# First attention batch pooled by TensorE from the local blocks' tiles, and the float64 words' shift on either of two engines

## The chip, the cores and the metric

The kernel runs on 1 core of one Trainium2 chip. The metric is the device time of one execution in microseconds (us). Engine names are short: PE is TensorE (PEld its weight loads), DVE is VectorE, ACT is ScalarE, POOL is GpSimd, SP is SyncE, whose queue starts the transfers (SPq).

## What is computed

Three parts follow each other; the output of one is the input of the next. The weights come as float64, and the kernel makes float32 of them itself.

```python
def attention(q, k, v):            # (4, 8, 576, 64); 4 batches, 8 heads, 576 tokens, 64 wide
    # pooled: mean of every 4 tokens of q, k, v, full softmax over 144 x 144, each row given to 4 tokens
    out_up = np.repeat(sm_attn(pool4(q), pool4(k), pool4(v)), 4, axis=2)
    # local: full resolution, but only keys at a distance under 4
    scores = np.where(np.abs(i - j) < 4, scale * q @ k.T, -1e9)
    return out_up + softmax(scores) @ v

def mixture1(x, w_in, w_out):      # x (2304, 512), w_in (512, 2048), w_out (2048, 512)
    h = x @ w_in
    return (h * np.cos(h)) @ w_out

def mixture2(x, w_gate, w_val, w_out, rms_g):   # 512 -> 1536 -> 512
    xn = x / rms(x) * rms_g
    return (silu(xn @ w_gate) * (xn @ w_val)) @ w_out
```

## The kernel before

The kernel is written as some hundred generators. A planner (`Order`, in the kernel itself) runs them while the program is built: each `yield` names an engine and an assumed duration, waits for an event, or takes a buffer from a pool, and the planner picks which generator issues next. What runs on the chip is the fixed order per engine that comes out, so an engine works strictly in that order and stands still when its next instruction waits. Where a `yield` lists two engines, the planner chooses the one that would be done first (a number behind an engine is a handicap).

**Attention, batch 0** (`start`, `pq_first`, `pv`, `pooled`, `block`, `block_v`). The pooled part has its own loads: q and k come in six pieces `pq` (tokens on all 128 partitions, four neighbours in a row; `pq_src`). The sums over four are made by DVE for q (L385) and in two adds by POOL for k (L380, L382), then PE transposes them (L425) and ACT writes them into the tiles `pqs` (L401). The pooled v has four loads `v` of its own (L480, L483), summed by POOL (L504 to L511) into `vh` and `vhl`. `pooled` makes the scores of a pair of heads (`sps`, L539), the softmax (L544 to L560), a transposition (`tra`, L575) and the product with v (`avp`, L594), whose result goes to `od` (L602).

The local part works in five blocks of 116 tokens. `block` loads the block's q and k (`raw`, L798, 256 KB each), transposes them (`btr`, L646, 4 instructions in the program for each), makes the scores (`bs`, L684, L690), the softmax (L699 to L712), a transposition (`bat`, L726), and the product with v (`bav`, L752) from the tiles `vb` (L814, four transfers of 64 KB a block, three buffers). L762 adds `od`, so no block can be finished ahead of the pooled part. L775 (ACT) and L777 (POOL) write the result into the tiles `big` as the two halves of x that mixture 1 reads. Batches 1 to 3 take the same path later, with tiles of their own (`rqk`, `pq`).

**Weights of mixture 1** (`w_loads`, `w_conv`). 32 pieces of 512 KB are loaded as pairs of 32-bit words (`rawwa`, `rawwb`, L291 and L293). A piece is converted in five steps: L316 on DVE shifts the low words right by 29, L320 on ACT rescales the high words, L322 on DVE puts both together, L324 on ACT makes the high half `wwa`/`wwb`, and L327 on POOL or DVE the low half.

**Mixture 1** (`unit`, `second`). x has nine tiles of 256 tokens. Tile 0 needs blocks 0 and 1 and the first 24 tokens of block 2; tile 1 needs the rest of batch 0 up to token 511; tile 2 the end of block 4 and the first two blocks of batch 1. A unit is two products `h` (L1013, 12 instructions each), the cosine (L1031 to L1049, ACT, DVE and POOL) and two products `y` (L1079, 6 instructions for each of two halves). Tiles 0 and 1 are run interleaved, 64 groups `h` and `y` together; each pair of units needs four weight pieces. `keep_warm` (L251) fills times in which the planner sees PE idle with products `warm` that nobody reads. Mixture 2 starts after that; its 36 weight pieces go through the same five steps in `w2_conv`.

`LOADS` sets the order of the first transfers on SP, after the six `pq`: four weight pieces, one block's q and k, the four `v`, one block, four weight pieces, three blocks.

Of the kernel before, what the change touches and what calls it, by code (L numbers as in the profile page):

```python
# [9 lines left out]
F32 = mybir.dt.float32  # L10
F32R = mybir.dt.float32r
I32 = mybir.dt.int32
ACTF = mybir.ActivationFunctionType
ALU = mybir.AluOpType
# [22 lines left out]
NQK, NV = 2, 3  # L37
LOADS = (("w", 4), ("r", 1), ("v", 0), ("r", 1), ("w", 4), ("r", 3))
# [11 lines left out]
NQS = 1  # L50
CVB, GLB = 9, 0.5
# [141 lines left out]
def fused_kernel(ctx: ExitStack, tc, q, k, v, w_in, w_out, w_gate, w_val, w_out2, rms_g, mask, bmask, out):  # L193
# [109 lines left out]

    def w_conv(m, i, raw, rp, r):
# [5 lines left out]
        w = p[1] if p[2] == "wg" else p[0].tile([128, 2, 512], F32R, tag=p[1], name="w" + p[1])  # L310
        raw = raw.rearrange("p (b c) -> p b c", c=2)
# [3 lines left out]
        a = yield "DVE", 0.34  # L315
        DVE.tensor_scalar(out=lw, in0=lw, scalar1=29, scalar2=None, op0=ALU.logical_shift_right)  # L316


# [57 lines left out]
    def sum4(b, w, t, o, n):  # L376

        if b or w:
            yield "POOL", 0.05 + n * 0.32
            POOL.tensor_tensor(out=t[:, :n, 0:2], in0=t[:, :n, 0:2], in1=t[:, :n, 2:4], op=ALU.add)  # L380
            yield "POOL", 0.05 + n * 0.18
            POOL.tensor_tensor(out=o, in0=t[:, :n, 0], in1=t[:, :n, 1], op=ALU.add)  # L382
        else:
            yield "DVE", 0.05 + n * 0.27
            DVE.tensor_reduce(out=o, in_=t[:, :n].rearrange("p u r d -> p u d r"), axis=AX.X, op=ALU.add)  # L385
# [28 lines left out]
    def pq_first(w, c, t, qs, place):  # L414

        u0, n = UC[c]
        yield wait(("pq", w, c))
        yield from sum4(0, w, t, qs[:, u0:u0 + n], n)
        give("pqp", place)
        yield take("att")  # L420
        i = yield take("bank")
        ps = bank_tile(i, [64, 4, 128], "trq")
        yield "PE", 0.2 * n
        for x in range(n):
            PE.transpose(ps[:, x, :], qs[:, u0 + x, :], ident)  # L425
        yield from pq_ev(0, w, c, ps)
        give("bank", i)
        give("att", "att")
        count(("pq", 0), 6)
# [57 lines left out]
    def pv(b, hp, t=None, place=None, vh=None):  # L487

        vi = 0
        if b == 0:  # L490
            yield wait(("pv", hp))
        else:
            vi = yield take("vh")
            vh = VH[vi]
            p = []
            for _ in range(2):
                x = yield take("pq")
                p.append(x)
            t = (ap.tile([128, 512], F32, tag=p[0], name="v4").rearrange("p (c x) -> p c x", c=2),
                 ap.tile([128, 512], F32, tag=p[1], name="v4")[:, :256])  # L500
            yield from pv_load(b, hp, *t)
# [10 lines left out]
        if b == 0:  # L512
            give(place[2], place)
        else:
            for x in p:
                give("pq", x)
# [3 lines left out]
    def pooled(b, hp, E=None):  # L520
# [72 lines left out]
        for c in range(3):  # L593
            PE.matmul(o, vh[:, c], A[:, c], start=c == 0, stop=c == 2)  # L594
# [35 lines left out]
    def block(b, u, raw, pools):  # L630
# [9 lines left out]
        for w in range(2):  # L640
# [4 lines left out]
            for a in range(4):  # L645
                PE.transpose(t[:, a, :], raw[w][:, 2 * a:2 * a + 2].rearrange("t h d -> t (h d)"), ident)  # L646
# [107 lines left out]
        give("vb", v_i)  # L754
# [46 lines left out]

    def block_v():

        for b in range(B):
            for u in range(5):
                S_.due(blk_due(b, u) - 5.0)
                x = yield take("vb")
                VI[b, u] = x
                r0 = geo(u)[2]
                vp = v[b].rearrange("(a e) t d -> e t a d", e=2)  # L810
                for s, (_, _, kc) in enumerate(groups(u)):
                    for e in range(2):
                        yield "SP", 0.5
                        SP.dma_start(VB[x][64 * e:64 * e + 64, s], vp[e, r0 + kc:r0 + kc + 64])  # L814
                done(("rv", b, u))
# [26 lines left out]
    def start():  # L842
# [3 lines left out]
        for n in [("pq", w, c) for c in range(3) for w in range(2)] + [("qs", w) for w in range(2)] + [("E", hp) for hp in (1, 2, 3)] \  # L846
                + [("v4", hp) for hp in range(4)] + [("vhl", 0)] + [("raw", u) for u in range(5)]:
            pl[n] = yield take(PLACES)
# [4 lines left out]
        def load(ev, us):  # L853
            yield "SP", us

        qs = [early(("qs", w), [128, 9, 64]) for w in range(2)]
        for c, (u0, n) in enumerate(UC):
            for w in range(2):
                t = early(("pq", w, c), [128, 4, 4, 64])
                yield "SP", max(0.48, 0.37 * n)  # L860
                SP.dma_start(t[:, :n], pq_src(0, w, u0, n))
                done(("pq", w, c))
                S_.add(pq_first(w, c, t, qs[w], pl["pq", w, c]), 0.0, S_.now())
# [984 lines left out]
```

## Time and profile before

| | us |
|---|---|
| runs (3), median | 983.76 (983.52 to 984.35) |
| the profiled execution, its own time | 984.96 |
| span of its records | 983.1 |
| PE busy | 953.0 (97% of the span) |
| DVE busy | 721.2 (73%) |
| ACT busy | 542.3 (55%) |
| POOL busy | 269.1 (27%) |

The span runs from the first to the last record of the execution; 1.9 us of its own time lie outside. Busy time of PE counts the products `warm` too, so it is not the same as useful work. Durations further on come from this one execution.

### The profile page before, as it was taken

What the parts mean: (1) busy time and instruction counts of PE and PEld (TensorE: products, weight loads), DVE (VectorE), ACT (ScalarE), POOL (GpSimd) and SP (SyncE); (2) the same over time, 40 slices, a digit from 0 to 9 for tenths busy, and PEclk for the clock granted to TensorE, in tenths of its full rate; (3) what the DMA queues carried; (4) which work ended last, traced back from release to release, by engine and by line L of the source; (5) the groups of instructions that cost most, each with busy time, mean ns of one, the idle gap of its engine ahead of it and who ended that gap; (6) DMA issues with size and microseconds to landing.
All of it is one profiled execution on the core that took longest, in us unless ns stands there. A gap on an engine that the chain in (4) does not pass through costs nothing.

```text
span 983.1 us, 19205 instructions
## 1 busy us (share of the span) xinstructions
PE 953.0 (97%) x7150; PEld 880.4 (90%) x7150; DVE 721.2 (73%) x1460; ACT 542.3 (55%) x1090; POOL 269.1 (27%) x325
## 2 busy tenths in 40 slices
PE   6789899999999999999999999999999999999998
PEld 6688778888988888888888889999999999999998
DVE  2789976677657775666577699586666688999895
ACT  3658886677677965656566465242322334554442
POOL 3877685544336311101042242000000014300000
PEclk9999999999999999999999999999999999999999
DMA  8788643567685554544331311133222144454432
GB/s 241 212 211 246 181 147 111 148 199 180 199 231 166 170 171 128 176 144 169 120 129 65 107 44 49 49 106 93 75 82 71 57 145 132 132 174 139 141 119 76
DMA packets 160333, 136.07 MB, mean 138 GB/s; under 512 B 72176, under 2 KB 133744, under 8 KB 160240
## 3 DMA queue, kind: packets, MB, share of 16 engines
q1 hardware_dynamic: 160240, 134.85, 45.8%
q8 instruction: 56, 0.92, 0.4%
q14 instruction: 37, 0.30, 0.1%
HBM read 98.64 MB, written 36.18 MB: 137 GB/s over the span
## 4 chain that ended last, share of the span: by engine, by line
PE 84%; DMA 4%; DVE 3%; SPq 3%; issue 2%; POOL 2%; ACT 2%; DVEq 0%; POOLq 0%; ACTq 0%
PE gvp L1502 26%; PE y L1079 19%; PE h L1013 18%; PE o L1755 13%; PE bav L752 2%; PE btr L646 1%; DMA pq<-in_q 1%; DMA raw<-in_k 1%; PE avp L594 1%; PE bs L690 1%; PE yt L1407 1%; POOL wwa L327 1%; PE bat L726 1%; PE sps L539 1%; DMA cst<-in_moe_rms_g 1%
## 5 line engine op out<-in xcount | busy, mean ns | idle before, releaser
L1502 PE MATMUL gvp<-xc,wc 128*128 128x384 f32 x1296 | 231.7, 335 | 0.0
L1502 PEld LDWEIGHTS gvp<-xc,wc 128*128 128x128 f32 x1296 | 225.6, 188 | 0.3
L1573 DVE TENSOR_TENSOR tmp<-gvp,tmp 128x384 f32<-128x384 f32 x180 | 99.3, 553 | 54.3 <-PE gvp L1502 51.0
L1013 PE MATMUL h<-big,wwa 128*128 128x256 f32 (+1 forms) x756 | 124.0, 316 | 0.9 <-DVE t L1038 0.5
L1755 PE MATMUL o<-wo,wc 128*128 128x256 f32 x972 | 118.4, 279 | 0.0
L1013 PEld LDWEIGHTS h<-big,wwa 128*128 128x128 f32 x756 | 107.5, 190 | 10.7 <-DVE t L1038 0.6
L1755 PEld LDWEIGHTS o<-wo,wc 128*128 128x128 f32 x972 | 115.7, 190 | 0.0
L1079 PE MATMUL y<-wwa,big 128*128 128x512 f32 x432 | 109.5, 397 | 0.7 <-DVE big L1049 0.7
L1079 PEld LDWEIGHTS y<-wwa,big 128*128 128x128 f32 x432 | 78.9, 188 | 17.7 <-DVE big L1049 1.6
L1013 PE MATMUL h<-big,wwb 128*128 128x256 f32 (+1 forms) x504 | 83.9, 317 | 0.4 <-DVE t L1038 0.3
L1079 PE MATMUL y<-wwb,big 128*128 128x512 f32 x324 | 82.0, 398 | 1.1 <-POOL big L1049 1.1
L1033 DVE SCALAR_TENSOR_TENSOR t<-kk,h 128x512 f32<-128x512 int32 x72 | 49.0, 681 | 44.1 <-ACT kk L1031 43.9
L1013 PEld LDWEIGHTS h<-big,wwb 128*128 128x128 f32 x504 | 72.0, 190 | 7.8 <-DVE t L1038 0.8
L1031 ACT ACTIVATE kk<-h 128x512 int32<-128x512 f32 x72 | 42.6, 592 | 58.1 <-PE h L1013 55.8
L1079 PEld LDWEIGHTS y<-wwb,big 128*128 128x128 f32 x324 | 59.0, 188 | 13.3 <-POOL big L1049 1.4
L1639 POOL TENSOR_TENSOR wt<-wo 128x256 f32<-128x256 f32 x10 | 9.8, 985 | 208.6 <-DVE wc L1358 183.4
L1038 DVE TENSOR_TENSOR t<-h,t 128x512 f32<-128x512 f32 x72 | 49.3, 686 | 17.9 <-ACT t L1036 17.4
L1564 ACT ACTIVATE tmp<-gvp 128x384 f32<-128x384 f32 x36 | 17.7, 492 | 75.8 <-PE gvp L1502 75.8
L1036 ACT ACTIVATE t<-t,cst 128x512 f32<-128x512 f32 x72 | 51.9, 722 | 13.4 <-DVE t L1033 12.9
L1047 ACT ACTIVATE big<-t 128x512 fp32r<-128x512 f32 x72 | 45.1, 628 | 25.1 <-DVE t L1038 23.7
L1698 ACT ACTIVATE wc<-ut 128x512 fp32r<-128x512 f32 (+1 forms) x60 | 34.3, 584 | 42.2 <-DVE ut L1684 25.3
L1049 DVE TENSOR_TENSOR big<-t,big 128x512 fp32r<-128x512 f32 x54 | 39.8, 738 | 16.6 <-ACT big L1047 16.3
(189 smaller groups left out, 1741.2 us busy)
## 6 DMA issues: line engine op xcount, KB each, us to landing
us<-tmp SPq DMA_DIRECT2D x72, 192.0 KB, 2.0
uf<-us SPq DMA_DIRECT2D x48, 256.0 KB, 3.0
rawwa<-in_moe_w_out SPq DMA_DIRECT2D x21, 512.0 KB, 4.3
wfs<-rawwa SPq DMA_DIRECT2D x36, 256.0 KB, 2.4
rawwa<-in_moe_w_gate SPq DMA_DIRECT2D x12, 512.0 KB, 4.3
rawwa<-in_moe_w_val SPq DMA_DIRECT2D x12, 512.0 KB, 4.6
wf<-wfs SPq DMA_DIRECT2D x12, 512.0 KB, 4.1
vb<-in_v SPq DMA_DIRECT2D x80, 64.0 KB, 2.8
```

The source lines that it names most:

```text
L1013: PE.matmul(h[:, w_ * ci:w_ * ci + w_], a[:, ksl], x_at(x, kk), start=m == 0, stop=m == 11)
L1031: ACT.activation(out=kk, in_=h, func=ACTF.Copy, scale=INV2PI, bias=0.25)
L1033: DVE.scalar_tensor_tensor(out=t, in0=kk, scalar=TWOPI, in1=h, op0=ALU.mult, op1=ALU.subtract)
L1036: ACT.activation(out=t, in_=t, func=ACTF.Sin, scale=-1.0, bias=cst[:, 0:1])
L1038: DVE.tensor_tensor(out=t, in0=h, in1=t, op=ALU.mult)
L1047: ACT.activation(out=gh, in_=t, func=ACTF.Copy)
L1049: (POOL if e == "POOL" else DVE).tensor_tensor(out=gl, in0=t, in1=gh, op=ALU.subtract)
L1079: PE.matmul(y[j][b], g[:, tsl], a, start=(first and ci == 0 and i == 0), stop=(last and c == 15 and i == 2))
L1502: PE.matmul(bank, w[:, a, kk], xc[:, x, b, kk], start=first and i == 0, stop=i == 5, skip_group_check=True)
L1573: DVE.tensor_tensor(out=half(o), in0=a, in1=half(b), op=ALU.add)
L1698: ACT.activation(out=o[:, 0], in_=src, func=ACTF.Copy)
L1755: PE.matmul(b[m][1][:, l], u[0][x][:, j, l], w[:, y, k], start=(p == 0 and l == 0 and i == 0), stop=(p == C3 - 1 and i == 2), skip_group_c ...
```

## The change

In batch 0 the pooled q, k and v no longer have loads of their own. The loads of the local blocks' q and k change their layout: a block's tile has heads of even and odd number on the two halves of the partitions, two neighbouring tokens in a row of 512 bytes, and comes in two transfers of 128 KB for q (SP) and two for k, which **ACT** issues. `sums` then multiplies the tile with a 0/1 matrix (`sel`, made once by POOL and DVE in `select`) on PE: 16 instructions in the program (L436 of the changed kernel) sum four tokens and transpose at once, into the bank `pq`; ACT or DVE copies it to `pqs`. `block` transposes the same tile with 16 instructions of half the size in place of 4 (L729). `vsums` does the same for v from the five tiles `vb` (two more of them, `vbx`): 24 instructions L474, and two copies to `vs`. `pooled` multiplies with `vs` by 6 instructions of 64 rows in place of 3. Gone are `pq_first`, the pooled loads, DVE's and POOL's sums, and POOL's sums for v. `LOADS` now mixes blocks, weight pieces and v one by one, and the due times of `pooled` (0 to -20) and `sums` (-40) put them first.

The shift by 29 becomes a choice of two engines (`shift`): DVE as before, or ACT, which reads the second 16-bit half of each word and rescales it. In the order that results ACT has 37 of the 68 shifts, 10 of the 32 of mixture 1's pieces.

```diff
-LOADS = (("w", 4), ("r", 1), ("v", 0), ("r", 1), ("w", 4), ("r", 3))
+LOADS = (("r", 1), ("w", 1), ("r", 1), ("w", 1), ("r", 3), ("v", 1), ("w", 1), ("v", 1), ("w", 1), ("v", 1), ("w", 1), ("v", 1), ("w", 1), ("v", 1), ("w", 4))
...
+SHB = 0.1
...
+    def shift(raw, lw):
+
+        _, e = yield [("DVE", 0.34), ("ACT", 0.6, None, None, SHB)]
+        if e == "ACT":
+            top = raw.bitcast(U16).rearrange("p (b c) -> p b c", c=4)[:, :, 1]
+            ACT.activation(out=lw, in_=top, func=ACTF.Copy, scale=2.0 ** -13, bias=2.0 ** -14 - 0.5)
+        else:
+            DVE.tensor_scalar(out=lw, in0=lw, scalar1=29, scalar2=None, op0=ALU.logical_shift_right)
...
-    def pq_first(w, c, t, qs, place):
...
+    def sums(u, raw):
+
+        _, n, _, off = geo(u)
+        m, j = n // 4, {0: 0, 3: 1, 16: 4}[off]
+        yield wait(("raw", 0, u))
+        yield wait("sel")
+        for w in range(2):
+            yield take("att")
+            i = yield take("bank")
+            ps = bank_tile(i, [128, 4, 29], "pq")
+            yield "PE", 0.9
+            for a in range(4):
+                for r in range(2):
+                    for e in range(2):
+                        pr = slice(64 * e, 64 * e + 64)
+                        PE.matmul(ps[pr, a, :m], raw[w][pr, a, r], M["q"][pr, r if off == 3 else 0, 32 * e + j:32 * e + j + m],
+                                  start=a == r == 0, stop=a == 3 and r == 1, skip_group_check=True)
+            t0 = (S_.cur["t"], "PE")
+            o, f = PQ[0][w][:, :, 29 * u:29 * u + m], (2.0 ** -7, 1.0)[w]
+            _, e = yield [("ACT", 0.22, t0), ("DVE", 0.2, t0, None, 0.3)]
...
+    def vsums(vs):
...
+        for u in range(5):
+            yield wait(("rv", 0, u))
+            yield "PE", 1.6
...
+                        PE.matmul(o, M["v"][pr, f, x:x + 64], VB[VI[0, u]][pr, s],
+                                  start=(c // 2, e) not in seen, stop=False, skip_group_check=True)
...
+    def select(t):
...
-                PE.transpose(t[:, a, :], raw[w][:, 2 * a:2 * a + 2].rearrange("t h d -> t (h d)"), ident)
+                if b:
+                    PE.transpose(t[:, a, :], raw[w][:, 2 * a:2 * a + 2].rearrange("t h d -> t (h d)"), ident)
+                    continue
+                o = t[:, a].rearrange("p (x r) -> p r x", r=2)
+                for r in range(2):
+                    for e in range(2):
+                        pr = slice(64 * e, 64 * e + 64)
+                        PE.matmul(o[pr, r], raw[w][pr, a, r], ident[pr, pr], start=a == r == 0, stop=a == 3 and r == 1, skip_group_check=True)
...
+        def raw_half(eng, t, src, u, us):
+            for e in range(2):
+                yield "SP" if eng is SP else "ACT", us
+                eng.dma_start(t[64 * e:64 * e + 64], flat(src, (e * S + geo(u)[2]) * 64, [[128, 64], [2 * S * 64, 4], [1, 128]]))
+
+        def raws(us):
+            for u in us:
+                t = early(("raw", u), [128, 2, 4, 2, 64])
+                o = t.rearrange("p w a r d -> p w a (r d)")
+                S_.add(raw_half(ACT, o[:, 1], k, u, 0.3), 0.0, 0.0)
+                yield from raw_half(SP, o[:, 0], q, u, 0.9)
+                done(("raw", 0, u))
+                S_.add(sums(u, (t[:, 0], t[:, 1])), -40, S_.now())
+                S_.add(block(0, u, (t[:, 0], t[:, 1]), (None, (pl["raw", u][2], pl["raw", u]))), blk_due(0, u), S_.now())
```

**Three places where the order changes.** First ACT, from its first instruction after `ident_r` on. Before, the mask tiles `bm` came behind the pooled copies `pqs`:

```order
L401 ACTIVATE pqs<-trq 64x64x4 x6
L401 ACTIVATE pqs<-trq 64x64 x2
L401 ACTIVATE pqs<-trq 64x64x4 x2
L401 ACTIVATE pqs<-trq 64x64 x2
L886 ACTIVATE bm<-bf 64x64 x2
```

Now (`raw_135` is block 0's tile, `raw_142` block 1's, `raw_205`, `raw_273`, `raw_320` those of blocks 2 to 4):

```order
L983 ACTIVATE bm<-bf 64x64 x2
L948 DMA raw_135<-in_k 64x4x128 x2
L948 DMA raw_142<-in_k 64x4x128 x2
L442 ACTIVATE pqs<-pq 128x4x29
L948 DMA raw_205<-in_k 64x4x128
L740 ACTIVATE bt<-btr 128x512
L948 DMA raw_205<-in_k 64x4x128
L442 ACTIVATE pqs<-pq 128x4x29
L740 ACTIVATE bt<-btr 128x512
L948 DMA raw_273<-in_k 64x4x128
L329 ACTIVATE rawwa_140<-rawwa_140 128x512
```

The mask tiles, which wait for a transfer, stand ahead of all loads of k, and the loads of blocks 2 and 3 stand between copies that wait for PE.

Second PE, where the pooled scores `sps` and the first sums of v lie. Before:

```order
L425 MATMUL trq<-ident,qs_108 64x128
L539 MATMUL sps<-pqs 72x144 x16
L646 MATMUL btr<-ident,raw_295 128x128 x4
L251 MATMUL warm<-ident 128x128 x3
L646 MATMUL btr<-ident,raw_295 128x128 x4
```

Now:

```order
L436 MATMUL pq<-sel,raw_320 64x29 x16
L474 MATMUL pv<-vb,sel 64x256 x4
L610 MATMUL sps<-pqs 72x144 x8
L474 MATMUL pv<-vb,sel 64x256 x6
L811 MATMUL bat<-ident,bE 128x128 x4
L729 MATMUL btr<-ident,raw_205 64x64 x16
L474 MATMUL pv<-vb,sel 64x256 x4
L610 MATMUL sps<-pqs 72x144 x8
L811 MATMUL bat<-ident,bE 128x128 x4
L474 MATMUL pv<-vb,sel 64x256 x6
```

The scores and the local blocks 0 and 1 now stand among products that wait for the loads of v; the last four `pv` come three rows further on.

Third PE again, at its first product of mixture 1. Before:

```order
L752 MATMUL bav<-bt,vb 64x58 x16
L646 MATMUL btr<-ident,raw_667 128x128 x4
L251 MATMUL warm<-ident 128x128 x3
...
L251 MATMUL warm<-ident 128x128
L1013 MATMUL h<-big,wwa_349 128x256 x12
L462 MATMUL trq<-ident,qs 64x128 x4
```

Now:

```order
L837 MATMUL bav<-bt,vb 64x58 x48
L729 MATMUL btr<-ident,raw_320 64x64 x16
L253 MATMUL warm<-ident 128x128 x4
...
L811 MATMUL bat<-ident,bE 128x128 x4
L253 MATMUL warm<-ident 128x128 x4
L837 MATMUL bav<-bt,vb 64x58 x16
L1102 MATMUL h<-big,wwa_209 128x256 x12
```

Three blocks are multiplied with v in one go (48 instructions), and block 3 is done too before mixture 1 starts; before, its `bav` followed after five groups `h`. Ahead of the first `h` the program has 36 products `warm` now, and had 108.

## Rows read from the trace of the kernel before

**Rows 1.** Busy time by stretch: us, PE, PEld, DVE, ACT, POOL, PEclk, DMA share, GB/s

```profile
20.00:70.00 50.00, 39.29 (x540) 35.64 (x538) 37.41 (x82) 31.97 (x90) 38.59 (x52) 1.00 0.82 224
...
0.00:70.00 70.00, 52.62 (x637) 48.37 (x637) 41.80 (x85) 36.63 (x100) 45.03 (x65) 1.00 0.81 224
70.00:160.00 90.00, 83.31 (x712) 73.35 (x711) 80.20 (x141) 73.92 (x143) 64.86 (x70) 1.00 0.62 180
200.00:983.00 783.00, 777.90 (x5443) 723.42 (x5441) 577.62 (x1197) 408.84 (x806) 141.61 (x167) 1.00 0.41 126
```

**Rows 2.** The same view for the products warm alone (L251 on PE)

```profile
0.00:69.87 69.87, 30.23 (x216) 1.00 0.81 224
69.87:160.00 90.13, 4.51 (x34) 1.00 0.62 181
```

**Rows 3.** Instructions of PE in order of time, from 21 us to the first h

```profile
21.69 2.48 PE L539 MATMUL sps<-pqs 64*72 64x144 f32 x32 [0.37 <-ACT pqs L401]
...
48.23 1.14 PE L752 MATMUL bav<-bt,vb 64*64 64x58 f32 x32
...
66.44 1.14 PE L752 MATMUL bav<-bt,vb 64*64 64x58 f32 x32
...
69.87 1.73 PE L1013 MATMUL h<-big,wwa 128*128 128x256 f32 x12
```

**Rows 4.** Who waited for whom, 0 to 70 us: total, times, longest

```profile
POOL pq L380 <- DMA pq<-in_k: 12.9, 2, 8.0
DVE qs L385 <- DMA pq<-in_q: 12.8, 3, 7.1
```

**Rows 5.** SP's issues in order of time: start, duration, transfer

```profile
14.83 0.60 SPq L291 DMA_DIRECT2D rawwb<-in_moe_w_in  x1
...
19.44 3.24 SPq L480 DMA_DIRECT2D v<-in_v  x1
...
33.52 0.59 SPq L798 DMA_DIRECT2D raw<-in_q  x1
```

**Rows 6.** Costliest groups of 0 to 70 us: total us, mean ns | idle before

```profile
L322 DVE SCALAR_TENSOR_TENSOR rawwb<-rawwb 128x512 int32<-128x512 int32 x8 | 6.5, 808 | 0.2 <-ACT rawwb L320 0.2
L316 DVE TENSOR_SCALAR rawwb<-rawwb 128x512 int32<-128x512 int32 x9 | 4.8, 545 | 0.0
L762 DVE TENSOR_TENSOR bt<-bav,od 64x464 f32<-64x464 f32 x6 | 3.8, 638 | 2.5 <-PE bav L752 2.4
L699 DVE TENSOR_REDUCE bst<-bs 128x4 f32<-128x256 f32 x8 | 3.3, 411 | 2.4 <-PE bs L690 2.4
L544 DVE TENSOR_REDUCE stat<-sps 72x2 f32<-72x288 f32 x8 | 3.0, 445 | 5.3 <-PE sps L539 5.3
L560 DVE TENSOR_TENSOR E<-E,stat 72x288 f32<-72x288 f32 x8 | 4.1, 553 | 0.4
L701 DVE TENSOR_TENSOR bE<-bs,bst 128x256 f32<-128x256 f32 x8 | 3.3, 418 | 0.1
L712 DVE TENSOR_TENSOR bE<-bE,bst 128x512 f32<-128x512 f32 x3 | 3.2, 1062 | 0.1
L707 DVE TENSOR_REDUCE bst<-bE 128x8 f32<-128x512 f32 x4 | 2.7, 681 | 0.5 <-ACT bE L705 0.4
```

**Rows 7.** DVE's first shift and block 2's transposition on PE, in order of time

```profile
31.87 0.42 DVE L316 TENSOR_SCALAR rawwb<-rawwb 128x512 int32<-128x512 int32 x1
...
64.68 0.66 PE L726 MATMUL bat<-ident,bE 128*128 128x128 f32 x4 [1.64 <-POOL bE L712]
```

**Rows 8.** Transfers of 0 to 80 us: count, size, median us to landing

```profile
vb<-in_v SPq DMA_DIRECT2D x24, 64.0 KB, 3.9
raw<-in_k SPq DMA_DIRECT2D x5, 256.0 KB, 5.1
bf<-band_mask SPq DMA_DIRECT2D x2, 36.0 KB, 3.3
```

More of the change, by code (lines that the diff above doesn't have):

```diff
@@ L314, in w_conv @@
         yield "ACT", 0.0
-        a = yield "DVE", 0.34
-        DVE.tensor_scalar(out=lw, in0=lw, scalar1=29, scalar2=None, op0=ALU.logical_shift_right)
+        yield from shift(raw2, lw)
         yield "ACT", 0.62
@@ L412, in count @@
             done(ev, XT[ev])
-    def pq_first(w, c, t, qs, place):
[L416 to L429, printed above, removed]
+    M = {}
@@ new lines, in sums @@
+    def sums(u, raw):
[17 more added lines that the diff above has]
+            _, e = yield [("ACT", 0.22, t0), ("DVE", 0.2, t0, None, 0.3)]
+            if e == "ACT":
+                ACT.activation(out=o, in_=ps[:, :, :m], func=ACTF.Copy, scale=f)
+            else:
+                DVE.tensor_scalar(out=o, in0=ps[:, :, :m], scalar1=f, scalar2=None, op0=ALU.mult)
+            give("bank", i)
+            give("att", "att")
+            done(("pq0", u, w))
+            count(("pq", 0), 10)
@@ L485, in pv_load, with pv @@
                 SP.dma_start(tb[64 * e + n:64 * e + 64], flat(v, f0 * 64, [[256, 64 - n], [1, 256]]))
[L487 to L501, printed above, removed]
+    def pv(b, hp):
+        vi = yield take("vh")
+        vh = VH[vi]
+        p = []
+        for _ in range(2):
+            x = yield take("pq")
+            p.append(x)
+        t = (ap.tile([128, 512], F32, tag=p[0], name="v4").rearrange("p (c x) -> p c x", c=2),
+             ap.tile([128, 512], F32, tag=p[1], name="v4")[:, :256])
+        yield from pv_load(b, hp, *t)
         ta, tb = t[0].rearrange("p c (r d) -> p c r d", r=4), t[1].rearrange("p (r d) -> p r d", r=4)
@@ L753, in block @@
         give("b2", a_i)
-        give("vb", v_i)
+        if v_i < NV:
+            give("vb", v_i)
+        else:
+            count("vb0", 2)
         t0 = (S_.cur["t"], "PE")
@@ L800, in fused_kernel, with load_v @@
     VI = {}
+    def load_v(b, u, x):
+        VI[b, u] = x
+        r0 = geo(u)[2]
+        vp = v[b].rearrange("(a e) t d -> e t a d", e=2)
+        for s, (_, _, kc) in enumerate(groups(u)):
+            for e in range(2):
+                yield "SP", 0.5
+                SP.dma_start(VB[x][64 * e:64 * e + 64, s], vp[e, r0 + kc:r0 + kc + 64])
+        done(("rv", b, u))
     def block_v():
-        for b in range(B):
+        yield wait(("rv", 0, 4))
+        for b in range(1, B):
             for u in range(5):
@@ L807, in block_v @@
                 x = yield take("vb")
[L808 to L815, printed above, removed]
+                yield from load_v(b, u, x)
     def blk_due(b, u):
@@ L932, in start @@
             S_.add(free_E2(x), 0.0)
-        yield wait(("E2", 2))
-        for _ in range(3):
-            p = yield take("pqp")
-            give(p[2], p)
     def free_E2(x):
@@ L1302, in w2_conv @@
         yield "ACT", 0.0
-        yield "DVE", 0.34
-        DVE.tensor_scalar(out=lw, in0=lw, scalar1=29, scalar2=None, op0=ALU.logical_shift_right)
+        yield from shift(raw, lw)
         yield "ACT", 0.62
```

142 lines of the change are left out of this document (88 added, 54 removed).

## The prediction

> **What bounds the kernel now.** I read the busy time by stretch first. From 200 us on PE is busy 777.90 of 783 us, and up to 70 us 52.62 of 70 [rows 1]. The reader is to see that the first number is a bound and the second is not: 30.23 us of the busy time ahead of the first group `h` are products `warm` [rows 2]. Without them PE did 52.62 - 30.23, about 22 us of work (a little more, since the durations overlap), in 70 us. So some 45 us are lost on PE at the start. Between 70 and 160 us it lost 90 - 83.31 = 6.7 us idle and 4.51 us `warm`, 11 us together. Later there is next to nothing: 5 us in 783. All that this change can win lies in the first 160 us.
>
> Then I read PE in order of time to see what the start waits for. The pooled scores come at 21.69 us, the first local product with v (which needs all of the pooled part) at 48.23, the third block's at 66.44, and `h` at 69.87 [rows 3]. The waits say why the scores are late: POOL and DVE wait 12.9 and 12.8 us for the pooled loads [rows 4]. Last I read DVE: its first shift of a weight word is at 31.87 us [rows 7], and it is busy 37.41 of the 50 us from 20 to 70 and 80.20 of the 90 from 70 to 160 [rows 1]. So there are two bounds in turn, loads and single waits up to about 30 us, then DVE. PE is the third, from about 160 us.
>
> **Term A, the first `h`.** The change moves DVE's conversion from behind the softmax to the front, and the start of `h` now depends on when DVE comes through its list. I count that list in the new order, up to the product `bE` of block 3, with the durations of [rows 6]: 9 merges (L322's kind) at 0.81 us make 7.3; 7 shifts at 0.55, 3.8; 8 maxima at 0.41 and 8 subtractions at 0.42, 6.6; 4 sums at 0.68, 2.7; 3 products `bE` at 1.06, 3.2; 8 pooled maxima, 3.0; 5 pooled products at 0.55, 2.8; 6 additions of `od` at 0.64, 3.8. Five copies of 512 elements I price like the sums, at 0.68, 3.4. The tail of small ones (reciprocals, two copies to `pqs`, `vs`, `at`) some 15 of them, I estimate at 4.5, at 0.3 each, under the 0.41 of the shortest row. The sum is 41 us, about what DVE did in all of the first 70 us before (41.80) [rows 1]. What it saves there is not work but idle time.
>
> When does it begin? ACT holds the first merge up. `bm` waits for the mask (issued by 2 us, 3.3 us to landing [rows 8]), so ACT issues k of block 0 from about 6 us, at 0.6 us for each half as on SP [rows 5]. It lands 3 to 5 us later (128 KB pieces; 5.1 for the old 256 KB [rows 8]), about 11. ACT's next copies wait for that, and the first weight piece's rescaling stands behind them, at about 13 us. From 13 us the 41 us end at 54 without any idle; I allow 3 us of waits. Then block 3's transposition, its copy and its product with v follow, 66.44 + 1.14 - 64.68 = 2.9 us before [rows 3, 7]. **`h` begins at about 60**, 9.9 us earlier. The ends: DVE begins at 9 us (k lands faster) and never waits, 9 + 41 + 2.9 = 53, a gain of 17; or it idles as it did from 20 to 70 us, 41 / (37.41 / 50) = 55, so 13 + 55 + 2.9 = 71, a gain of nothing. I lean to the middle because much of that old idle time belongs to waits for the pooled v that go away.
>
> What must be ready besides DVE: v of block 4. SP has 38 issues up to it; at 0.60 us each (512 KB) or 0.59 (256 KB) [rows 5] that is 23 us if nothing holds them up, and a landing of 3.9 [rows 8] gives 27. One issue took 3.24 us in a full queue [rows 5]; I allow four such, +11, so `vs` comes between 28 and 38 us. DVE's list reaches it only at about 36, so its cost is zero unless the queue is worse than that. Halving the q loads adds 5 issues, 3 us, which lie in this sum. The Trainium skill (DMA: Bandwidth & Descriptors, Rules for kernel authors) advises against just this: two transfers to two halves of the partitions serialize, and one should be used. The nearly equal 0.59 and 0.60 us agree that an issue costs the same whatever its size; by the rule the change pays those 3 us for no bandwidth, and here they are covered.
>
> **Term B, work added on PE.** Ten sums `pq`, the smaller transposes and 24 products for v are more PE instructions than the transposes that go, but all lie ahead of `h`, where PE loses 45 us; they cost nothing unless DVE's list shrinks to less than PE's. Behind `h` something goes: block 3's `bav` (1.14 us [rows 3]) and `bat` (0.66 [rows 7]) are done ahead now, against one transposition of batch 1 that falls behind. Gain 1.2 us.
>
> **Term C, 70 to 160 us.** Of the 80.20 us of DVE there, the change takes out block 3's and most of block 4's softmax (about 5 us by the same rows), 6 shifts that ACT does now (3.3), and two whole pieces that are converted ahead (2 x 1.35 = 2.7): 11 us. ACT gets 6 x 0.6, with 73.92 of 90 us busy, so it stays under DVE. The PE loss of 11 us in that stretch was partly DVE's and partly tile 1 that was not ready; block 3 no longer is late. I take 5 us off, with 0 and 10 as ends.
>
> **Term D, later.** Of the shifts, 27 of mixture 2's move to ACT. PE is busy 777.90 of 783 there with DVE at 577.62 and ACT at 408.84 [rows 1], so PE covers them: 0, with 1 us either way for the new order.
>
> Sum: 9.9 + 1.2 + 5 = 16 us. The profiled execution took 984.96 us of its own time, 1.2 over the median of 983.76; its 969 become 968 against the median.
>
> **Rivals.**
> 1. *More comes through.* DVE begins at 9 us, and POOL (45.03 us busy in the first 70 [rows 1]) is rid of the pooled sums, its durations fall, and the 11 us of 70 to 160 nearly vanish. 17 + 1.2 + 8 = 26: 958. For it: PE, DVE and POOL all lose work or idle time. Against: the loads of k hang on ACT's order.
> 2. *ACT's queue eats the start.* ACT issues ten loads of k between copies that wait for PE. If four of them stall like SP's 3.24 us, ACT stands for 11 us, and with it rescaling, exponentials and all of DVE's list; `h` comes at about 69 and only 3 to 5 us of B and C remain: about 979. For it: that row. Against: the queue was full behind eight transfers of weights and q, k; here the k loads come before most weights.
> 3. *Slower.* PE works in order, and the last `pv` stands ahead of the scores of block 2. If v of block 4 comes late, everything behind it waits. The point from which it decides is a landing after about 45 us, 9 past DVE's need, since 10 us of A are then gone; at one us per issue, about what SP needed while its queue was held up, and with some stalls of 3.24 us, it lands at 52, `h` at 76, six later than now, and little of C is left: 988. For it: 24 products that all wait for SP's slowest kind of issue (64 KB each). Against: SP has no waits for buffers left ahead of them.
> 4. *It does not do what it says.* The pooled part gets earlier but block 2's own chain sets `h` again (its transposition was at 64.68 us [rows 7], long after `od`). Then the start stays near 68 us and C is small: 982 to 985.
>
> **How the numbers follow.** A measurement of this kernel tells about 0.2% (2 us) from no change. My forecast, 962 to 975, has a chance of 0.55; rival 1 0.18, rival 2 0.14, rival 4 0.06, rival 3 0.07. Faster by over 0.2% comes from the forecast, rivals 1 and 2 and a small part of rival 4: 0.88. Within 0.2%: 0.05; slower: 0.07. The range runs from rival 1 to rival 2, 956 to 979; about 2 in 10 are left out, beyond both ends.
>
> **What would show it.** Right: first `h` between 55 and 65 us; DVE's first shift near 10 us and its first merge near 13; `sps` about 21 to 24 us, hardly earlier than before; idle plus `warm` of PE from 70 to 160 at 4 to 8 us; the stretch from 200 us to the end unchanged within 1 us, once shifted. Wrong: ACT standing behind its own issues (rival 2); PE waiting at the `pv` for v while block 2's scores are ready (rival 3); PE idle again near the end of tiles 0 and 1, because in the new order batch 1's first local products come after 60 of their 64 groups, where 45 preceded them, so that tile 2 is late. With 108 products `warm` cut to 36, a granted clock below 1.00 (the lower level of 1.2 GHz) in the first 60 us would lengthen PE's pieces there; every stretch before shows 1.00 [rows 1], so I give it no price.

## The result: the changed kernel is slower

The changed kernel takes 997.74 us (median of 5 runs, 995.45 to 1000.4), the kernel before 983.57 (5 runs beside it, 983.43 to 984.35): a ratio of 1.0144, 95% interval 1.0123 to 1.0164. It is 14 us slower; 16 us of gain were predicted. Here and below a median takes in all runs, while a ratio leaves out one run of `x2` (999.24 us, over 1.5% above that kernel's fastest) and is not the plain quotient of the two medians. The profiled execution took 996.03 us of its own time, its span is 993.9.

**The profile after: where the time went.** PE in order of time, in the changed kernel (start, duration, instruction, and in brackets the idle time before it and what ended it):

```profile
12.78 0.30 PE L436 MATMUL pq<-sel,raw 64*64 64x29 f32 x2 [1.47 <-DMA raw<-in_k]
15.84 1.80 PE L436 MATMUL pq<-sel,raw 64*64 64x29 f32 x29 [2.77 <-DMA raw<-in_k]
...
30.47 6.99 PE L436 MATMUL pq<-sel,raw 64*64 64x29 f32 x128
...
42.59 2.20 PE L610 MATMUL sps<-pqs 64*72 64x144 f32 x16
...
80.78 1.46 PE L1102 MATMUL h<-big,wwa 128*128 128x256 f32 x10
```

Against [rows 3]: the scores `sps` come at 42.59 us in place of 21.69, the first `h` at 80.78 in place of 69.87. From the first `h` to the end of the span it was 983.1 - 69.87 = 913.2 us before and is 993.9 - 80.78 = 913.1 now. So the whole loss lies ahead of `h`, and what was to be won behind it is not there either.

The same kernel's busy time by stretch (us, PE, PEld, DVE, ACT, POOL, granted clock, DMA share, GB/s):

```profile
0.00:14.00 14.00, 10.24 (x108) 9.75 (x108) 2.08 (x9) 2.76 (x7) 4.63 (x14) 1.00 0.78 178
14.00:16.00 2.00, 0.16 (x4) 0.17 (x4) 0.00 (x0) 0.27 (x1) 0.00 (x0) 0.51 1.03 196
16.00:30.00 14.00, 14.00 (x250) 13.37 (x252) 2.54 (x6) 5.25 (x11) 1.29 (x1) 0.50 1.00 210
30.00:44.00 14.00, 14.00 (x228) 12.60 (x226) 6.19 (x15) 3.19 (x7) 2.04 (x2) 0.50 0.85 224
...
20.00:70.00 50.00, 46.32 (x785) 39.55 (x784) 31.29 (x73) 25.90 (x78) 11.55 (x10) 0.72 0.56 140
```

The last line answers to the first of [rows 1]. PE, which was to have slack there, is busy 46.32 of 50 us, and DVE, which was to be the bound, 31.29, less than before. The four lines above it say when: after the two waits for k PE stands almost still from 14 to 16 us, the granted clock falls to 0.50 (1.2 GHz), and then PE is busy without a gap for 28 us at that level. One group of 32 sums `pq` takes 1.12 us at a clock of 1.00 and 1.87 at 0.50. Meanwhile DVE does 2.54 us of work in 14.

Why k is late stands in ACT's order of time (ACTq is its DMA issues):

```profile
3.46 0.94 ACT L983 ACTIVATE bm<-bf 64x64 fp32r<-64x64 f32 x4 [0.27 <-DMA bf<-band_mask]
5.76 8.83 ACTq L948 DMA_DIRECT2D raw<-in_k  x4
14.64 0.27 ACT L442 ACTIVATE pqs<-pq 128x116 f32<-128x116 f32 x1 [10.23 <-DMA raw<-in_k]
...
20.21 0.66 ACT L329 ACTIVATE rawwa<-rawwa 128x512 f32<-128x512 f32 x1
22.12 0.27 ACT L442 ACTIVATE pqs<-pq 128x116 f32<-128x116 f32 x1 [1.25 <-PE pq L436]
22.13 2.38 ACTq L948 DMA_DIRECT2D raw<-in_k  x3
```

The first issue does start at 5.76 us, as predicted. But four issues of 0.60 us each are spread over 8.83 us in which ACT does nothing else, and the last three of ten come from 22.13 to 23.9 us. In the program each of these issues carries a wait for one of eight completion semaphores, which the transfers of SP and ACT share in turn: an issue waits until the transfer that had its semaphore before has landed. The trace shows that this wait is what holds ACT's first four issues:

| issue of k starts | its semaphore | transfer that had it before | issued | us to landing | landed |
|---|---|---|---|---|---|
| 5.76 | DMAHW3 | SP, second half of block 0's q | 2.71 | 3.0 | 5.7 |
| 8.63 | DMAHW5 | SP, first half of block 1's q | 4.02 | 4.6 | 8.6 |
| 12.42 | DMAHW7 | SP, a weight piece | 5.32 | 7.1 | 12.4 |
| 13.99 | DMAHW1 | SP, second half of block 2's q | 6.60 | 7.4 | 14.0 |

What stands behind is in DVE's order of time: its first shift is at 8.29 us (near 10 was predicted), and then it waits 12.18 us for ACT's rescaling L329, which stands behind the issues and copies of k:

```profile
8.29 0.43 DVE L313 TENSOR_SCALAR rawwa<-rawwa 128x512 int32<-128x512 int32 x1 [4.07 <-DMA rawwa<-in_moe_w_in]
20.90 0.69 DVE L331 SCALAR_TENSOR_TENSOR rawwa<-rawwa 128x512 int32<-128x512 int32 x1 [12.18 <-ACT rawwa L329]
```

**Behind the first `h`.** I set both kernels side by side, first over 90 us from their own first `h` on, then from 200 to 400 us. The kernel before, by stretch:

```profile
69.87:160.00 90.13, 83.44 (x712) 73.48 (x712) 80.33 (x141) 74.05 (x144) 64.95 (x71) 1.00 0.62 181
...
200.00:400.00 200.00, 199.86 (x1840) 177.59 (x1839) 138.19 (x273) 143.94 (x279) 72.90 (x99) 1.00 0.64 182
```

The changed kernel, by stretch, and then for its products `warm` alone (L253):

```profile
80.78:171.00 90.22, 85.16 (x681) 74.37 (x678) 75.36 (x122) 78.11 (x138) 66.26 (x68) 1.00 0.63 184
...
200.00:400.00 200.00, 195.89 (x1883) 173.49 (x1882) 132.70 (x264) 152.18 (x297) 74.33 (x113) 1.00 0.68 196
...
80.78:171.00 90.22, 2.33 (x18) 2.18 (x18) 1.00 0.63 184
```

In the first 90 us PE lost 6.69 idle + 4.51 `warm` [rows 2] = 11.2 us before and loses 5.06 + 2.33 = 7.4 now: 3.8 won. Between 200 and 400 us it was idle 0.14 us before and is idle 4.11 now: 4.0 given back.

### The profile page after: what moved, and what is told of

Read it like the earlier page. It is cut to its first block, busy times and chain, and to the rows that moved or that the text cites. A ratio compares the mean times of both kernels' runs of the same rounds, so it can differ in the third digit from the quotient of the medians.

```text
span 993.9 us, 20057 instructions
## 1 busy us (share of the span) xinstructions
PE 968.3 (97%) x7634; PEld 890.2 (90%) x7634; DVE 705.5 (71%) x1431; ACT 563.1 (57%) x1125; POOL 244.3 (25%) x295
## 4 chain that ended last, share of the span: by engine, by line
PE 78%; DVE 7%; DMA 6%; ACT 4%; issue 2%; SPq 1%; POOL 1%; DVEq 0%; ACTq 0%; POOLq 0%
PE gvp L1590 25%; PE y L1168 15%; PE h L1102 14%; PE o L1843 13%; PE bav L837 2%; PE pq L436 2%; DMA wfs<-rawwa 2%; DMA rawwa<-in_moe_w_gate 1%; PE btr L729 1%; PE sps L610 1%; DMA v<-in_v 1%; PE btr L723 1%; PE avp L666 1%; DMA raw<-in_k 1%; PE bs L775 1%
## 5 line engine op out<-in xcount | busy, mean ns | idle before, releaser
L1168 PEld LDWEIGHTS y<-wwb,big 128*128 128x128 f32 x324 | 59.1, 188 | 14.9 <-DVE big L1138 1.6
L1138 DVE TENSOR_TENSOR big<-t,big 128x512 fp32r<-128x512 f32 x58 | 43.0, 741 | 13.9 <-ACT big L1136 13.3
```

Of the source, the lines that this page charges most:

```text
L1138: (POOL if e == "POOL" else DVE).tensor_tensor(out=gl, in0=t, in1=gh, op=ALU.subtract)
L1168: PE.matmul(y[j][b], g[:, tsl], a, start=(first and ci == 0 and i == 0), stop=(last and c == 15 and i == 2))
```

## The experiments

Four questions stay. Is the late start the loads, or the clock that fell after them? Is it ACT's queue that makes the loads late, or their number and order? What does the choice of engine for the shift do? And where does an early `h` go? The kernels ran on two chips, each group with the kernel before beside it: 985.26 us (19 runs) for `x1`, `x2`, `x3` and `x7`, 984.65 (27) for `x4`, `x9`, `x10`, `x11`, 984.47 (28) for `x5`, `x12`, `x13`, `x14`. Unless said otherwise an edit is made to the changed kernel.

### x1_warm: the clock kept up

```diff
             i = yield take("bank")
+            if u == 0 and w == 1:
+                own = bank_tile(i, [128, 128], "warm")
+                for _ in range(32):
+                    PE.matmul(own, ident, ident, start=True, stop=True, skip_group_check=True)
             ps = bank_tile(i, [128, 4, 29], "pq")
```

> 32 more products warm on PE just ahead of the sums of block 0's k, where PE of the changed kernel waits 4.2 us for that load; nothing else moves. Theory C (clock: after the wait PE runs at 0.50 from 14 to 44.5 us and its many small products are then the bound): granted clock 1.00 from 14 to 45 us, a group of 32 records pq about 1.1 us and not 1.9, the scores sps at 33 to 36 us and not 42.6, the first h at 72 to 75 us and not 80.8, time 988 to 992. Theory L (the loads of k and v are the bound, the clock only fills waiting time): clock 1.00 too, but sps no earlier than 40 us, h within 2 us of 80.8, time 995 to 1000.

1001.14 us, ratio 1.0175 (1.0131 to 1.0219). By stretch:

```profile
16.00:30.00 14.00, 12.19 (x339) 11.39 (x338) 3.04 (x7) 3.18 (x8) 0.15 (x1) 0.98 0.99 217
30.00:44.00 14.00, 12.28 (x164) 10.09 (x166) 7.95 (x18) 6.03 (x18) 3.74 (x3) 0.53 0.93 248
```

The clock stays at 0.98 up to 30 us. PE then comes through its sums faster than k arrives, waits for k again between 28 and 32 us, and the clock falls after that. The scores come at 40.84 us, 1.75 earlier, `h` at 79.06. So keeping the clock up does not cure the late loads (theory L); the filling itself took 7.41 us of PE. What the fall of the clock costs by itself `x1` does not show, for its edit moves more than the expectation says: in the program the last four issues of k now stand seven or eight places later in the turn of the semaphores, and they start at 24.83 to 28.4 us, where they started at 19.55 to 23.9.

### x2_kSP: k issued by SP

```diff
-                eng.dma_start(t[64 * e:64 * e + 64], ...
+                SP.dma_start(t[64 * e:64 * e + 64], ...
```

> The ten transfers of k are issued by SP in the places that the planner meant for them, instead of by ACT; every engine's other order is the same. Theory Q (ACT's order and its mask wait delay k): k of block 0 lands by 7 us and not 12.8 to 15.8, ACT's stretch of issues from 5.8 to 14.6 us is gone, PE has no wait at 11 to 16 us and keeps its clock, sps at 32 us, h at 70, time 984 to 988. Theory S (an issue waits for the transfer eight places before it, whoever issues it, and twenty halves use the places up): block 0 lands early, but k and q of blocks 2 to 4 land no earlier than before the edit (24 to 29 us), v of block 4 as late as 39 us, PE still has a wait and loses its clock, h at 76 to 80 us, time 992 to 998.

992.1 us (983.65 to 999.24), ratio 1.0057 (1.0025 to 1.0088). DMA issues of line L948 (count, shortest/median/longest in ns, first and last start in us), in the changed kernel:

```profile
L948 SPq DMA_DIRECT2D raw<-in_q x10: 595/605/815, 2.0 to 13.4; - x10
L948 ACTq DMA_DIRECT2D raw<-in_k x10: 602/602/734, 5.8 to 23.9; - x10
```

and here, followed by PE in order of time:

```profile
L948 SPq DMA_DIRECT2D raw<-in_k x10: 596/616/650, 2.0 to 15.8; - x10
L948 SPq DMA_DIRECT2D raw<-in_q x10: 596/616/1384, 2.7 to 17.2; - x10
...
27.29 1.20 PE L610 MATMUL sps<-pqs 64*72 64x144 f32 x16
...
65.72 3.13 PE L1102 MATMUL h<-big,wwa 128*128 128x256 f32 x24
```

Busy time by stretch:

```profile
16.00:30.00 14.00, 13.23 (x356) 11.47 (x353) 10.45 (x24) 6.62 (x20) 3.25 (x3) 1.00 0.75 185
30.00:44.00 14.00, 12.08 (x227) 9.51 (x227) 11.80 (x28) 11.16 (x40) 5.74 (x7) 1.00 0.94 264
...
200.00:400.00 200.00, 192.02 (x1775) 169.28 (x1774) 132.68 (x263) 152.26 (x295) 69.67 (x103) 0.99 0.66 192
```

The same twenty transfers, all issued by one engine, are out by 17.2 us in place of 23.9. PE never waits for k, the clock is 1.00 from 16 to 44 us, the scores come 15.3 us earlier and `h` 15.1 us earlier, 4.2 ahead of the kernel before. It is the queue (theory Q), though Q's numbers missed: `h` is earlier than its 70 us, the time above its 984 to 988. The Trainium skill (DMA: Bandwidth & Descriptors, Rules for kernel authors) says that spreading transfers over SP and ACT doesn't help bandwidth and only saves issue time. On bandwidth the traces agree: from 2 to 36 us the core moved 206 GB/s with two queues and 205 with one. Issue time two queues did not save here; they cost 6.7 us until the last issue. But the time does not follow `h`: it is still above the kernel before. From 200 to 400 us PE is idle 200 - 192.02 = 8.0 us.

### x7_warm_kSP: both

> Both edits at once: k issued by SP, and 32 products warm ahead of block 0's k. Theory C with Q: clock 1.00 throughout, h at 68 to 70 us, time 982 to 986. Theory L or S: h at 75 us or later, time over 988.

999.01 us, ratio 1.0131 (1.0086 to 1.0177); `h` at 75.46. With the loads in time the filling only delays: 9.7 us later than `x2`. Nor does it keep the clock: PE waits for no load, and the granted clock is 0.50 from 30 to 36 us all the same.

### x5_loads_first: all q and k ahead of weights and v, k still on ACT

```diff
-LOADS = (("r", 1), ("w", 1), ("r", 1), ("w", 1), ("r", 3), ...
+LOADS = (("r", 5), ("w", 2), ("v", 1), ("w", 1), ...
```

> The changed kernel with one line of another table: all ten q halves and ten k halves of batch 0 are issued before any weight or v piece; k stays on ScalarE's queue. Theory P (each issue waits for the transfer eight places earlier, and two engines that issue in turn hold each other up): the k issues are still spread out, 8 us or more from the first to the fourth and the tenth not before 20 us (23.9 in the changed kernel, 16.2 with k on SyncE); TensorE waits for k again, its granted clock falls to 0.50 before 20 us, the last pooled sum is after 35 us. Rival O (it is the other transfers, weights and v, between them that delay k): tenth k issue by 16 us, sums done by 28 us at a clock of 1.00. The weights come later in either case, so the first h is 70 or later under both, and the time 985 to 1002.

994.43 us, ratio 1.0093 (1.006 to 1.0127). ACT in order of time:

```profile
3.44 0.93 ACT L983 ACTIVATE bm<-bf 64x64 fp32r<-64x64 f32 x4 [0.40 <-DMA bf<-band_mask]
7.30 12.31 ACTq L948 DMA_DIRECT2D raw<-in_k  x8
...
19.71 1.26 ACTq L948 DMA_DIRECT2D raw<-in_k  x1
21.01 0.63 ACTq L948 DMA_DIRECT2D raw<-in_k  x1
```

and SP's issues of that time:

```profile
2.02 6.58 SPq L948 DMA_DIRECT2D raw<-in_q  x10
8.64 0.61 SPq L293 DMA_DIRECT2D rawwa<-in_moe_w_in  x1
9.29 0.50 SPq L295 DMA_DIRECT2D rawwa<-in_moe_w_out  x1
11.59 6.42 SPq L898 DMA_DIRECT2D vb<-in_v  x4
```

Eight issues now stand one behind the other on ACT with no other work between them, and they still take 12.31 us where 8 x 0.60 = 4.8 would do; the tenth is at 21.01, and PE's clock is 0.50 from 16 to 30 us. That is theory P's picture, though its number for the sums missed (the last began at 30.6 us, not after 35). Rival O doesn't fall cleanly: the table puts weights and v behind k, but SP, done with q at 8.6 us, sends two weight pieces ahead of seven of the ten k issues and four v ahead of the last four all the same. So this is what the run shows: on two queues SP runs ahead of k whatever the table says, and on one queue (`x2`) the table's order holds. The wait is the same as in the changed kernel: ACT's seventh issue starts at 18.32 us, and the weight piece whose semaphore it waits for, issued by SP at 9.29, took 9.0 us to land. So the shared semaphores hold ACT's issues. Why landings take 3.0 to 9.0 us there, with the DMA share at 0.96 to 1.16, no run separates.

`h` comes at 69.62 us, 11.2 earlier than in the changed kernel, and yet the time is above the kernel before. The planner's order of every engine moves with the table, so this gain is not the loads' alone.

### x3_shift_only: the kernel before with the choice of engine for the shift alone

```diff
(kernel before)
-        DVE.tensor_scalar(out=lw, in0=lw, scalar1=29, scalar2=None, op0=ALU.logical_shift_right)
+        yield from shift(raw, lw)
```

> The kernel before with the choice of engine for the shift alone, nothing of the attention part. Theory N (the shift is worth little): 981 to 984.5, first h at 67 to 70 us. Theory D (DVE bounds 70 to 160 us, the shift takes it off): PE idle plus warm from 70 to 160 us falls from 11 to 5 us, time 976 to 980. Rival (ACT becomes the bound, or late products of mixture 2 wait for it): 985 or more.

988.09 us (983.45 to 990.55), ratio 1.0026 (1.0008 to 1.0044). `h` is 3.0 us earlier, and then 3.7 us are idle from 200 to 400, where the kernel before had 0.14. The profile is of the fastest of the ten runs. The time is the rival's, whose cause (ACT as the bound, or late products of mixture 2) no row here shows. The first line is PE's, the second is the stretch:

```profile
66.87 1.84 PE L1024 MATMUL h<-big,wwa 128*128 128x256 f32 x12
...
200.00:400.00 200.00, 196.30 (x1792) 172.06 (x1796) 129.94 (x251) 150.90 (x291) 73.28 (x102) 1.00 0.64 183
```

### x4_no_shift, x9_kSP_noshift2, x10_kSP_noshift: the shift taken out of the change

`x4` gives every shift back to DVE, k stays on ACT:

```diff
-        _, e = yield [("DVE", 0.34), ("ACT", 0.6, None, None, SHB)]
+        _, e = yield [("DVE", 0.34)]
```

> The changed kernel with all 68 shifts on DVE again; the attention part as changed, the planner's order after the start moves with it. Theory A (the shifts on ACT cost PE 4 us of idle time from 200 to 400 us, since there ACT's copies and exponentials stand behind them): h stays at 80 us, idle of PE from 200 to 400 us falls from 4.1 to under 1 us, time 992 to 996. Rival (that idle time comes from the late start and the late loads, not from the shifts): idle stays at 3 to 4 us, time as the changed kernel, 996 to 1000.

991.11 us, ratio 1.0067 (1.0045 to 1.009); `h` at 73.61, 7.2 us earlier than in the changed kernel. Theory A missed twice: `h` moved, and the idle time from 200 to 400 us stays at 3.8, as the rival had it. `x10` is `x4` with k on SP; `x9` has k on SP and the choice for mixture 1's pieces only.

> k issued by SP and all shifts on DVE: the attention part of the change alone, with its loads mended. Theory A: first h at 64 to 68 us as with k on SP alone, idle of PE from 200 to 400 us under 1 us (8 us with the shifts on ACT), time 978 to 983. Rival (the earlier start is lost to batch 1 coming late whatever the shifts do): 984 to 990 with idle of 4 us or more between 160 and 400 us.

> k issued by SP, the choice of engine kept for the 32 pieces of mixture 1 (10 on ACT), DVE alone for the 36 of mixture 2. If the 27 late shifts on ACT are what costs: idle of PE from 200 to 400 us under 1.5 us and the time within 2 us of the kernel with all shifts on DVE. If the 10 early ones cost too: 3 us or more over it.

`x10`: 980.35 us (975.45 to 985.82), ratio 0.9956 (0.9927 to 0.9985), below the kernel before. `x9`: 986.84, ratio 1.0027 (0.9997 to 1.0058), `h` at 67.44: 6.5 us over `x10`, so the ten early shifts on ACT cost too. `x10`'s PE in order of time, then by stretch:

```profile
28.00 1.21 PE L610 MATMUL sps<-pqs 64*72 64x144 f32 x16
...
49.92 2.96 PE L837 MATMUL bav<-bt,vb 64*64 64x58 f32 x96
...
58.70 5.99 PE L1102 MATMUL h<-big,wwa 128*128 128x256 f32 x48
...
20.00:40.00 20.00, 19.25 (x393) 15.16 (x393) 15.85 (x41) 11.38 (x45) 5.16 (x5) 1.00 0.77 200
40.00:58.00 18.00, 16.89 (x390) 15.08 (x388) 16.93 (x37) 11.99 (x29) 11.36 (x11) 1.00 0.60 185
...
200.00:400.00 200.00, 196.96 (x1840) 173.33 (x1839) 144.14 (x282) 141.25 (x280) 67.48 (x97) 1.00 0.66 188
```

The start is now the one that I had predicted: `h` at 58.70, with DVE busy 16.93 of the last 18 us ahead of it. Its idle time from 200 to 400 us, 3.0, is not theory A's. And at `h` the causes add up: against the changed kernel's 80.78, k on SP alone wins 15.1, DVE's shifts alone 7.2, both together 22.1 (one profile each). `x4` and `x10` differ in k's queue alone, and there too it is worth 14.9 us at `h`, and 10.8 us in the time.

Why the choice costs 7 us at the start is seen when `x2` and `x10` are compared, which differ in it alone. Who PE waits for in `x2` from 38 to 66 us, and below it two of DVE's instructions there:

```profile
PE avp L670 <- DVE at L655: 2.0, 1, 2.0
PE bs L769 <- DVE vs L485: 1.6, 1, 1.6
...
41.00 2.94 DVE L313 TENSOR_SCALAR rawwb<-rawwb 128x512 int32<-128x512 int32 x1 [0.39 <-DMA rawwb<-in_moe_w_in]
43.86 0.41 DVE L485 COPY vs<-pv 128x256 f32<-128x256 f32 x1
```

In `x10` PE's waits from 38 to 59 us have in place of these two:

```profile
PE avp L670 <- ACT at L653: 0.2, 1, 0.2
```

The planner balances the two engines by assumed durations. With shifts on ACT it moves one of the two copies `vs` over to DVE, and the one `at` that DVE makes in either kernel is a later one (at 49.49 us, at 43.33 in `x10`). There `vs` stands behind a shift that takes 2.94 us from its start to its end, where the others take 0.42, just as its weight piece comes in; and `bav` begins at 55.22 in place of 49.92. The new order also puts block 3's `bav` ahead of `h`. These two waits are 3.4 of the 7 us; the rest is not worked out.

### x11_kSP_noshift_vhold: batch 1's v tiles later

```diff
-        yield wait(("rv", 0, 4))
+        yield wait(("h", 2))
```

> As the kernel with k on SP and all shifts on DVE, and the loads of v for batch 1 are not taken up before the third unit of mixture 1, so that SP does not stand 14 us behind a tile that is still in use while no transfer runs. Theory V (that standstill delays the weight pieces and costs PE from 70 to 120 us): DMA share from 47 to 70 us over 0.5 and not under 0.2, PE idle plus warm from the first h to 120 us at least 2 us less, time 2 to 4 us less than without. Rival (DVE bounds that stretch, the loads wait anyway): within 1 us.

981.55 us, ratio 0.998 (0.9954 to 1.0006). PE's idle time of 200 to 400 us goes, 0.65 us in place of 3.0 in `x10`, but 3.0 us turn up from 120 to 160, where `x10` has none. By stretch:

```profile
200.00:400.00 200.00, 199.35 (x1860) 176.56 (x1859) 145.77 (x283) 143.62 (x276) 71.26 (x98) 1.00 0.64 184
120.00:160.00 40.00, 36.96 (x239) 32.03 (x238) 30.07 (x56) 30.96 (x66) 34.31 (x38) 0.96 0.33 97
```

The wait is moved, not removed. Theory V's sign is missing: the DMA share from 47 to 70 us is 0.52, and was 0.55 in `x10` already.

### x14_kSP_noshift_again, x13_kSP_noshift_fill, x12_kSP_noshift_FR1: what the clock takes

`x14` is `x10` again; the other two are `x10` with more filling products.

```diff
(x13)
-FT2, FR2 = 215, 0.6
+FT2, FR2 = 215, 1.0
...
-        if n < 1 or t0 > FT2 or t0 > FT and t1 - t0 < 0.8:
+        if n < 1 or t0 > FT2 or t0 > FT and t1 - t0 < 0.3:
(x12)
-FR = 0.8
+FR = 1.0
```

> The kernel of the earlier run that was below before (k issued by SyncE, every shift on VectorE), run again beside the two fillers: 976 to 986, ratio 0.992 to 0.999, first h at 57 to 60 us. If the earlier gain was the chip's scatter alone, the ratio's interval takes in 1.

> The same kernel with ten more filling products of 128x128 where TensorE would stand idle between 90 and 215 us; the order of the rest is the same. Theory C (what is lost between first h and end is largely the clock that falls at 70 to 80 and 120 to 140 us after short waits): clock 1.00 in 120 to 160, and 1 to 3 us below the same kernel without them. Rival (the clock's dips after 90 us cost under 0.5 us, the loss is the waits at 200 to 400): within 1 us of the kernel without them, or slower by the 2 us that ten fillers last.

> The same kernel with the filling up to 90 us at 1.0 of the planned idle time in place of 0.8 (58 filling products in all in place of 46); the planner then also puts some of the later work in another order. Theory C: mean granted clock 0.99 or more and 1 to 4 us below the same kernel with 0.8. Rival: no gain, and any change of order is worth up to 6 us either way, as between the variants before; then first h and the idle of 200 to 400 tell which.

`x14`: 979.97 us (975.74 to 986.49), ratio 0.9962 (0.9938 to 0.9985): the gain of `x10` is there again. `x13`: 985.58, ratio 1.0004 (0.998 to 1.0027). `x12`: 980.59, ratio 0.9969 (0.9944 to 0.9994). Ten more fillers made the kernel slower (5.6 us in the median), and 0.8 or 1.0 makes no difference to the time, though in the profile of `x12`, a slower one of its runs (986.31), `h` is at 64.50. `x13` did not even keep the clock: 0.92 from 120 to 140 us. In these two forms filling does not help; the theory that it would give 1 to 4 us falls.

But the time goes with the clock. `x14`'s profile, by stretch and PE's first `h`:

```profile
16.00:30.00 14.00, 13.23 (x347) 11.66 (x343) 8.46 (x19) 4.90 (x12) 2.25 (x2) 0.82 0.78 188
...
120.00:140.00 20.00, 18.70 (x138) 16.70 (x139) 14.66 (x31) 17.19 (x31) 13.23 (x18) 0.83 0.22 68
...
61.09 6.00 PE L1102 MATMUL h<-big,wwa 128*128 128x256 f32 x48
```

This is the same program as `x10`, whose clock was 1.00 from 16 to 30 us, and `h` is 2.4 us later. Over `x14`'s 12 runs the mean granted clock of a run lies between 0.983 and 0.998, and the time follows it: 986.26 us at 0.983, 975.74 at 0.998. In which stretches the other eleven runs lost it is not shown. The kernel before lies at 0.992 or above in all its runs beside these experiments, 0.997 on average; `x14` at 0.990 on average.

## Why the prediction was wrong, step by step

| kernel | first `h` | span less that |
|---|---|---|
| before | 69.87 | 913.2 |
| changed | 80.78 | 913.1 |
| x4: DVE shifts | 73.61 | 913.2 |
| x2: k on SP | 65.72 | 918.5 |
| x10: both | 58.70 | 914.8 |
| x14: the program of x10 again | 61.09 | 916.6 |
| x5: all q and k first | 69.62 | 922.8 |
| x7: k on SP and 32 more `warm` | 75.46 | 923.3 |
| x3: before with the choice | 66.87 | 914.8 |

- **Term A failed.** The step is "ACT issues k of block 0 from about 6 us, at 0.6 us for each half as on SP": the start was right (5.76), the pace was not. The term has no wait of an issue for the landing of one of SP's transfers; with it four issues took 8.83 us in place of 2.4. Block 0's two halves then landed 7.0 and 7.2 us after their issue, not 3 to 5, the second at 15.8 us in place of 11, and the first merge came at 20.90 us, not 13. The sign hangs on this and on the choice of the shift together: with k on SP alone (`x2`) or with DVE's shifts alone (`x4`) the kernel is still slower than before, with both (`x10`) it is faster. The ends that I gave for `h`, 53 to 71 us, held only for DVE's list. The size of that list was nearly right: I counted 41 us, and DVE is busy 43.02 us ahead of `h` in the changed kernel. That `x10`'s `h` (58.70) lies so near my 60 is in part luck: DVE is busy 38.41 us ahead of it there, all its shifts are DVE's, and in `x14` the same program has `h` at 61.09.
- **The failing clause of Term B** is that PE's added products "cost nothing unless DVE's list shrinks to less than PE's". PE had no slack: it was busy without a gap from 16 to 44 us at half the clock. I had named a clock below 1.00 and given it no price. By the rows it is 0.75 us for each group of 32 sums, 7.5 us for the ten groups, if all ran at 0.50. How much of this price lies on the path to `h` no run shows: in `x1` the clock was up until 30 us, but k's last issues came later too, PE waited for k instead, and `h` gained 1.7 us. The gain of 1.2 us does not show either: summed over the stretches behind `h`, PE's work without `warm` is 893.8 us now and was 892.6, not less.
- **Term C came near in size:** 3.8 us of the 5 came in the first 90 us behind `h`. That they came from DVE's relief is not shown: DVE did 5.0 us less there (75.36 against 80.33), not 11, and 2.2 of the 3.8 are products `warm` that are no longer there. What I did not see is that 4.0 go again from 200 to 400 us.
- **Term D failed.** 0 with 1 us either way was argued from busy shares. `x3` measures the choice on its own: 2.6 us slower (ratio 1.0026), with 3.7 us idle at 200 to 400. At the start it was not the shift's duration but the order that the planner made of it (`x2` against `x10`); what it is at 200 to 400 is open. That idle time is not the choice's alone: `x4` has 3.8 and `x10` 3.0 without it.
- **SP's half of the queue** cost nothing, as I had said, but in part by luck: the last transfer of block 4's v was issued at 35.06 us and took 4.5 us to land, 39.6 where I gave 38 as the upper end, and it was in time because all else was late. In the changed kernel no wait of PE names v. My warning from the Trainium skill (DMA: Bandwidth & Descriptors, Rules for kernel authors) was on halved transfers as such; no run here has whole ones, so their part isn't shown.
- **The rivals.** Rival 2 had the place, ACT's queue, and not the size: it gave 979 for `h` at 69. The queue was late by more: PE waited 4.2 us for k and DVE 12.18 behind ACT, and the choice of the shift took 7 us more. Rival 3's wait for v did not occur.
- **A mended start is not worth its size.** `x10` wins 11.2 us at `h` and in the median some 4 at the end (980.35 against 984.65). Some 1.6 us go in the profiled execution's stretch behind `h`. That execution (975.45 us) is the fastest of the ten; the rest goes in the other runs, whose clock is lower. Why the stretch behind `h` varies from 913 to 923 us with the order is open.

## What to carry to other kernels

Before a load is moved to a second engine's queue, count not its issue time but what the other queue will have put ahead of it by then, and look in the program for what each issue waits for; here one queue, which kept the order of need, was faster than two. A stage that gets many small matrix products must be priced at both clock levels wherever one late load stands ahead of them. And when a planner is given a new choice, read where it puts the work that makes room, for here the start came 7 us later by the order that it made of the choice.

## What the runs showed of the hardware that was not expected

- ScalarE issued eight transfers in 12.31 us with nothing between them, though one issue takes 0.60 (`x5`): in this program an issue waits for the landing of an earlier transfer, which can be SyncE's (5.76 us after a landing at 5.7, 12.42 after one at 12.4 in the changed kernel). SyncE issued the same kind twenty times from 2.0 to 17.2 us with two weight pieces between (`x2`).
- After waits of 1.47 and 2.77 us TensorE's granted clock fell to 0.50 and stayed there from 14 to 44 us, though the engine was busy 28.00 of the 28 us from 16 on with small products (most of them 64x29 and 64x64). In `x10`, with the same products and no wait over 0.8 us, it was 1.00 from 16 to 44 us. But such waits are not the whole of it: in `x14`, the same program with no wait over 0.7 us, it was 0.58 from 24 to 30 us, and in `x7` 0.50 from 30 to 36. The Trainium skill (TensorE: Matmul & The Clock Gate, What's actually happening) says that activity releases the throttle; 28 us of unbroken work at the low level differ from that, and the measurement decides.
- The same program runs at mean clocks from 0.983 to 0.998, and its time lies 10.5 us lower at the upper end (`x14`).
